# Laying out every engine's work anew in a planned attention + FFN kernel, with the planner's durations taken from a trace

## The chip, the cores and the metric

The kernel runs on one core of one Trainium2 chip. A core has five engines that run side by side, each working through its own instructions in the order in which they were written: TensorE (PE in the profile; PEld is its loading of weights, which overlaps), VectorE (DVE), ScalarE (ACT), GpSimd (POOL) and SyncE (SP), which here only issues DMAs. An instruction that waits for a semaphore holds up everything behind it on its engine. The metric is the device time of one launch in microseconds (us); lower is better. Before the change it is 315.80 us, the median of three runs (315.71 to 315.86).

## The reference

Attention in which a query sees only the keys of its own cluster, then a gated feed-forward network (FFN). There are 4 batches of 8 heads with 768 positions of 64 values, 16 centroids for each head; the FFN goes from 512 to 1536 and back on 3072 tokens.

```python
q_assign = np.argmax(np.einsum('bhsd,hcd->bhsc', q_n, c_n), axis=-1)
k_assign = np.argmax(np.einsum('bhsd,hcd->bhsc', k_n, c_n), axis=-1)
mask = q_assign[:, :, :, None] == k_assign[:, :, None, :]
scores = np.where(mask, scale * np.matmul(q, k.transpose(0, 1, 3, 2)), -1000000000.0)
...
attn = attn / (np.sum(attn, axis=-1, keepdims=True) + 1e-09)
x = np.matmul(attn, v)  # heads side by side: 3072 x 512
gate = 1.0 / (1.0 + np.exp(-(x @ w_gate)))
val = x @ w_val
out = gate * val @ w_out
```

## The kernel before

**The work of one pair of heads.** Heads go in pairs p = 0 to 3 of each batch b. Queries, keys and values come in by DMA (`dma`, line 323) into nine tiles "nat". Queries and keys are turned so that the 64 values lie on the partitions: in batch 0 and the first pairs of batch 1 by TensorE transposes (lines 881 for pair 0, 773 for pairs 1 to 3 of batch 0, 595 for pairs 0 and 1 of batch 1) whose result DVE or ACT copies out of PSUM (L555 on DVE, L780 on ACT), otherwise by DVE in blocks (`turn_blocks`, L573). TensorE then scores them against the centroids in float32 (L926, L813; L665 for two pairs at a time). DVE turns these scores (L527), takes the largest (L534), matches it (L541: which centroid has the largest score) and turns the one-hot rows back, straight into the operands as mask rows (L552) or into a tile that DMAs spread. POOL casts the turned queries and keys to float16 (L801, L628, L895) into "even" and "odd" tiles; from batch 1 on a DMA shifts the second head's half into "odd" (L632). The operands have 80 rows then: 64 values and 16 one-hot rows, so that one matmul gives score and mask together. POOL also casts the values (L499).

**Attention** (`attend`). The scores of a unit (L986, 256 or 384 columns) go into one of two PSUM buffers "sc"; ACT takes the exponential of a whole buffer (L1010, 768 or 1024 elements) into one of four "es" tiles; TensorE multiplies these with the values and a column of ones (L1037, 65 columns), which gathers in one PSUM buffer "av" the sums and their divisor. At the end of a block of queries DVE takes the reciprocal (L1062) and multiplies (`norm`, L1067) into "xn", which is turned into x by a DMA transpose on SP (L1095) or by TensorE (L1075) with a copy by DVE (L1091).

**FFN** (`feed`, `project`). For each half of a batch's tokens, 12 steps of a gate and a value product (L1372: four matmuls each, into three PSUM buffers "ring"), a tanh on ACT in place of the sigmoid (L1390), and DVE's product into hT (L1401). The output projection is done on 2 by 2 blocks with seven products (L1252), with sums of weights (L1145 to L1151, DVE), of hT (L1221, DVE), and scalings and sums of the products (L1277 ACT, L1283, L1287, L1325 DVE, L1298 ACT, L1304 and L1308 POOL). The FFN of one half runs between the attention of later ones, so that TensorE always has something.

**What sets the order.** Nothing is emitted where it stands in the code. Each piece is a task: engine, duration, what it waits for, the buffers that it takes and uses, a due time, an earliest time, and `lat`, which is how long after its end its readers may start. `Order.schedule` plans all engines together in the planner's own time. On each engine, of the tasks that could start within 0.02 us of the first, the one with the smallest due time goes next:

```python
first = min(c[0] for c in cand)
start, t = min(
    (c for c in cand if c[0] <= first + 0.02), key=lambda c: (c[1].due, c[0])
)
```

The planned starts are the order in which the instructions are emitted, and so the order of each engine's queue and the choice of buffers. On the chip only this order remains: durations and due times have no effect of their own. Due times come from `due_at(slot)` for attention (a slot is a score unit, 96 in batch 0) and `due_ffn(work)` for the FFN (`work` counts its TensorE time); the many small offsets (for instance 3.5 and -23.5 at the value product) move one kind of task against another.

Of the kernel before, what the change touches and what calls it, by code (L numbers as in the profile page):

```python
# [12 lines left out]
ALU = mybir.AluOpType  # L13
# [187 lines left out]
def kernel(  # L201
# [204 lines left out]
    c4 = od.add("DVE", 1.65, c_scale, [c1], due=-8.8, seq=[c2])  # L406
# [85 lines left out]
    def load_v(b, p, eng, due, due_cast, early=0.0, behind=()):  # L492
        i = b * NP + p
        load_nat(b, p, "v", eng, due, early, behind=behind)
        buf = natb[b, p, "v"]
        vload[b, p] = [
            od.add(
                "POOL", 0.5,
                lambda e=e: nc.gpsimd.tensor_copy(  # L499
                    vps[i % NVP][:, e, :, 0:D], buf.tile[:, e, :, :]  # L500
                ),
                nat[b, p, "v"] + [ones[i % NVP]] + last_av.get((i - NVP, e), []),
                due_cast, uses=[buf],
            )
            for e in range(2)
        ]
# [50 lines left out]
    def prepare(b, grp, due, step, act=(), queues=("SP",), split=False):  # L557
# [5 lines left out]
        for p, nm in sides:  # L563
            t32[p, nm] = Buf("t32")
            for half in range(2):
                if quarters(b, p):

                    def turn_blocks(p=p, nm=nm, half=half):
# [10 lines left out]
                        "DVE", 0.55, turn_blocks, nat[b, p, nm], due, lat=0.15,  # L579
# [20 lines left out]
                def copy(p=p, nm=nm, half=half, rb_=rb_):  # L600
# [11 lines left out]
                    "ACT" if (nm, half) in act else "DVE", 0.5, copy,  # L612
                    [tr], due, lat=0.15, uses=[rb_, t32[p, nm]],
# [4 lines left out]
        for p in grp:  # L618
            ev, od_ = aug[b, p] = Buf("even"), Buf("odd")
            prev = []  # L620
            for half in (0, 1) if split else (None,):
# [13 lines left out]
                for nm in ("k", "q"):  # L635
                    first = not prev and not c
                    c.append(
                        od.add(
                            "POOL", 0.83 * part, lambda nm=nm, cast=cast: cast(nm),
                            [cp[p, nm, h] for h in hs], due, seq=(prev + c)[:1],  # L640
                            acq=[ev] if first else [],
                            uses=[t32[p, nm]] + ([] if first else [ev]),
                        )
                    )
# [29 lines left out]
        for half in range(2):  # L674
# [10 lines left out]
            def back(cols=cols, oh=oh, half=half):  # L685
# [4 lines left out]
                "DVE", 0.53,  # L690
                lambda t1=t1, half=half: turn_scores(take(t1)[:n], rg.tile[:n, half, :QB]),
                [cl], due, acq=[t1], uses=[rg],
            )
            a2 = od.add(
                "DVE", 0.52,
                lambda t1=t1, mx=mx: top_scores(take(mx)[:n], t1.tile[:n]),
                [a1], due, acq=[mx], uses=[t1], lat=0.0,
            )
            a3 = od.add("DVE", 0.55, same, [a2], due, acq=[oh], uses=[t1, mx], lat=0.0)
            if quarters(b, grp[0]):  # L700
                a3 = od.add("DVE", 0.25, weigh, [a3, c_small], due, uses=[oh], lat=0.0)
            a5 = od.add(
                "DVE", 0.38, back, [a3], due, seq=turned[-1:],
# [24 lines left out]
    def place(b, p, ohf, tiles, last, due, alloc, c):  # L728
# [6 lines left out]
        for n_, (e, nm, h) in enumerate(rows):  # L735
            g = tiles.index((nm, h))
            m = od.add(
                "DVE", 0.395,
                lambda g=g, e=e, nm=nm, h=h: turn_matches(
                    aug[b, p][e].tile[64:96, NM[nm], h * QB : (h + 1) * QB],  # L740
                    ohf.tile[32 * g : 32 * g + 32, 32 * e : 32 * e + QB],
                ),
                [last, *alloc], due + 0.3 * n_ + (0.0 if n_ > 5 else 0.0), uses=[ohf, aug[b, p][e]],
            )
            masked[b, p, e, nm, h] = [c[nm, e, h], m]
# [11 lines left out]
    def prepare_pair(b, p, due, step, act=("q",), direct=False):  # L757
# [3 lines left out]
        for h in range(2):  # L761
            for nm in ("k", "q"):
# [15 lines left out]
                def copy(nm=nm, cols=cols, rg=rg):  # L778
# [12 lines left out]
                    "ACT" if nm in act else "DVE", 0.5, copy, [tr], due, lat=0.15, uses=[rg, t32[nm]]  # L791
# [4 lines left out]
        for nm, e in (("k", 0), ("q", 0), ("k", 1), ("q", 1)):  # L796
            to = od_ if e else ev

            def cast(nm=nm, e=e, to=to):
# [4 lines left out]
                "POOL", 0.83, cast, [cp[nm, 0], cp[nm, 1]], due + 0.1 * e,  # L804
# [58 lines left out]
    def prepare_first(due):  # L863
# [8 lines left out]
        for nm, h in (("k", 0), ("k", 1), ("q", 0), ("q", 1)):  # L872
# [34 lines left out]
            cp[nm, h] = od.add(on, 0.5, copy, [tr], due, lat=0.1, uses=[rg, t32[nm]])  # L907
# [30 lines left out]
        for dur, go, acq, uses in (  # L938
            (0.58, lambda: turn_scores(take(t1), rg.tile[:, :QB]), t1, [rg]),
            (  # L940
                0.55,
# [19 lines left out]
    def attend(block, at, slot):  # L961
# [13 lines left out]
        early = slot < 108.0  # L975
# [28 lines left out]
        def exponentials():  # L1004
# [16 lines left out]
            "ACT", 0.13 + 0.00078 * together * N, exponentials,  # L1021
            [*t1, c_small, c3], due, lat=0.2, acq=[es], uses=[sc],
# [8 lines left out]
        def value():  # L1031
# [15 lines left out]
            due + (-4.1 if last else 3.5) - (23.5 if early else 0.0), lat=0.25 if last else 0.0,  # L1047
# [52 lines left out]
        t4 = od.add("DVE", 0.17 + 0.02 * nq, rec, [t3], due - 18.0, lat=0.05, acq=[rr], uses=[av])  # L1100
        t5 = od.add("DVE", 0.14 + 0.15 * nq, norm, [t4], due - 18.0, lat=0.2, acq=[xn], uses=[av, rr])
        if not ((b, gr) == (0, 0) and p >= 2 or (b, p) == (0, NP - 1) or block == blocks[-1]):
# [3 lines left out]
                    "SP", 1.4, turn_by_dma, [t5], due - 18.0, seq=xd[:1], lat=0.0 if b else 5.0, dma=0.4,  # L1106
# [4 lines left out]
        t6 = od.add("PE", 0.02 + 0.06 * nq, turn, [t5, c_ident16], due - 18.0, lat=0.25, acq=[rg], uses=[xn])  # L1111
        xd.append(
            od.add(
                "DVE", 0.1 + 0.133 * nq, out_of_bank, [t6], due - 18.0, lat=0.2, seq=xd[:1],
# [12 lines left out]
    def sum_weights(due):  # L1127
# [26 lines left out]
        for kind, dur in (("1112", 0.84), ("2122", 0.84), ("1122", 0.42)):  # L1154
# [10 lines left out]
    def project(b, one, two, final, many, end):  # L1165
# [45 lines left out]
        def add(to, place, x, y, op, behind=()):  # L1211
            tasks = []
            for n, (i0, i1) in enumerate(parts):
# [4 lines left out]
                        "DVE", 0.15 + 0.067 * (i1 - i0),  # L1218
# [7 lines left out]
                        due - -10.0 - (6.0 if end and not n else 0.0), lat=0.15, acq=fresh,  # L1226
# [16 lines left out]
        def product(ring, bank, new, lo, hi, left_, right, deps, acq, uses, n0=0, runs=((0, NFC // 2),)):  # L1243
# [33 lines left out]
            "ACT", 0.4, first(fresh_hf, lambda: nc.scalar.mul(t_hf(), t_r1()[:, HM:], 0.5)), [m2], due, lat=0.2,  # L1277
# [4 lines left out]
            "DVE", 0.42,  # L1282
# [4 lines left out]
            "DVE", 0.42, lambda: stt(t_hf(), t_r2()[:, HM:], 0.5, t_df()[:, 1], ALU.mult, ALU.add),  # L1287
# [6 lines left out]
        def mixed():  # L1294
# [3 lines left out]
            "ACT", 0.6, lambda: nc.scalar.mul(mixed(), t_r1(), 0.5), [m5, m4], due_ffn(work()), lat=0.2,  # L1298
# [4 lines left out]
            eng, 0.42 if eng == "DVE" else 0.65,  # L1303
# [4 lines left out]
            eng, 0.42 if eng == "DVE" else 0.65, lambda: add_on.tensor_tensor(t_df()[:, 0], t_df()[:, 0], t_hf(), ALU.add),  # L1308
# [12 lines left out]
        if not end:  # L1321
            m7 = product(r2, t_r2, False, 0, HM, lambda: a(0, 1), lambda i: views["2122"][:, i], a7, [], hs)
            e5 = od.add(
                "DVE", 0.68,
# [10 lines left out]
            "DVE", 0.42, lambda: stt(o2.tile[:, 1, HM:], t_r2()[:, HM:], 0.5, t_df()[:, 1], ALU.mult, ALU.add),  # L1335
# [9 lines left out]
        for lo, hi in zip(cuts, cuts[1:]):  # L1345
# [5 lines left out]
                "DVE", 0.12 + 0.3 * (hi - lo) / HM,  # L1351
# [7 lines left out]
    def feed(b, gr, work):  # L1359
# [24 lines left out]
        for fc in range(NFC):  # L1384
# [4 lines left out]
                "ACT", 0.12 + 0.3 * w,  # L1389
# [3 lines left out]
                [g1, c3], due, lat=0.2, acq=[gt], uses=[rg],  # L1393
# [4 lines left out]
            def gated(fc=fc, rv=rv, gt=gt):  # L1398
# [8 lines left out]
                    "DVE", 0.1 + 0.4 * w, gated, [g2, v1], due - 15.0, lat=0.2, seq=done[:1],  # L1407
# [12 lines left out]
        if not wsum_done:  # L1420
            sum_weights(93.0)
# [22 lines left out]
    for p_ in range(1, NP):  # L1444
# [17 lines left out]
    for p_ in range(1, NP):  # L1462
        prepare_pair(0, p_, (0, 9.5, 13.5, 18.5)[p_], 0.24, (('k', 'q'), (), ('k', 'q'))[p_ - 1], p_ in (1, 2, 3))
# [75 lines left out]
```

## Time and profile before

| what | value |
|---|---|
| median of 3 runs | 315.80 us (315.71 to 315.86) |
| the profiled execution's own time | 315.89 us |
| its span | 314.1 us, so 1.8 us lie around it |
| PE busy | 307.8 us (98%), 3083 matmuls |
| ACT busy | 221.3 us (70%) |
| DVE busy | 206.0 us (66%) |
| POOL busy | 93.4 us (30%) |
| DMA | 36.83 MB, mean 117 GB/s |
| granted TensorE clock | 0.999 |

A line of the timeline reads: start in us, duration, engine, line and operation, output<-inputs, shape and type, how many in a row, and in brackets the idle time before it with what ended it. In the chain that ended last a line is start, length and what ran. Matmuls overlap their neighbours, so the length of one is longer than what it costs in a row; the start-to-start step of equal matmuls is the cost. A queue's lines (SPq) are DMAs, with the time the engine spent to issue them, waits included.

### The profile page before, as it was taken

How to read it: one execution, taken by the hardware profiler on the slowest of the kernel's cores; microseconds unless marked ns; L12 is line 12 of the kernel's file. 1: busy time of each engine (PE TensorE's matmuls, PEld its weight loads, DVE VectorE, ACT ScalarE, POOL GpSimd, SP SyncE). 2: the span in 40 equal slices, each digit the busy share in tenths (PEclk: the TensorE clock that was granted, in tenths of full speed). 3: DMA queues.
4: the chain of work that ended last, by engine and by line, in shares of the span. 5: the costliest groups of instructions: out<-in, count | busy, mean ns of one | idle time of the engine just before them, and what ended most of it. 6: DMA issues, size and time to landing. Idle time of an engine off the chain costs nothing.

```text
span 314.1 us, 7876 instructions
## 1 busy us (share of the span) xinstructions
PE 307.8 (98%) x3083; PEld 213.3 (68%) x3083; DVE 206.0 (66%) x480; ACT 221.3 (70%) x323; POOL 93.4 (30%) x140
## 2 busy tenths in 40 slices
PE   8999999999999999999999999999999999999995
PEld 4567888545668866567666876657766787667674
DVE  4999733899979659485335899576333753457684
ACT  4699999237999767777788857767788777632321
POOL 4998659551014224420202135430210021000000
PEclk9999999999999999999999999999999999999999
DMA  6999999957175669521574649631310012000103
GB/s 221 374 220 251 216 211 168 187 121 131 42 114 88 143 121 263 147 77 37 120 113 71 103 78 234 176 83 40 88 57 13 15 61 100 3 0 12 58 2 134
DMA packets 79957, 36.83 MB, mean 117 GB/s; under 512 B 64512, under 2 KB 74864, under 8 KB 79920
## 3 DMA queue, kind: packets, MB, share of 16 engines
q1 hardware_dynamic: 72048, 24.30, 33.1%
q0 software_dynamic: 6864, 11.01, 17.6%
q10 hardware_dynamic: 1008, 1.02, 0.9%
q8 instruction: 24, 0.39, 0.5%
q14 instruction: 13, 0.11, 0.1%
HBM read 28.34 MB, written 6.29 MB: 110 GB/s over the span
## 4 chain that ended last, share of the span: by engine, by line
PE 91%; DVE 7%; issue 1%; ACT 0%; DVEq 0%; ACTq 0%
PE ring L1372 40%; PE sc L986 18%; PE ring L1252 14%; PE av L1037 10%; PE sc L665 3%; PE sc L1252 3%; DVE even L552 2%; DVE odd L552 1%; PE av L348 1%; DVE t L527 1%; DVE ohf L541 1%; PE ring L881 1%; DVE mx L534 1%; DVE t L555 1%; PE ring L595 1%
## 5 line engine op out<-in xcount | busy, mean ns | idle before, releaser
L1010 ACT ACTIVATE es<-sc,nbias 128x768 f16<-128x768 f32 (+1 forms) x189 | 167.1, 913 | 34.6 <-PE sc L986 33.1
L1401 DVE SCALAR_TENSOR_TENSOR hT<-gt,ring 128x384 f16<-128x384 f32 (+2 forms) x96 | 53.0, 552 | 58.9 <-PE ring L1372 55.0
L1372 PE MATMUL ring<-x,wv 128*128 128x384 f16 (+2 forms) x384 | 78.1, 326 | 0.0
L1372 PE MATMUL ring<-x,wg 128*128 128x384 f16 (+2 forms) x384 | 78.1, 326 | 0.0
L1390 ACT ACTIVATE gt<-ring 128x384 f32<-128x384 f32 (+2 forms) x96 | 47.1, 490 | 35.1 <-PE ring L1372 20.9
L1037 PEld LDWEIGHTS <-es 128*128 128x128 f16 x1152 | 55.1, 97 | 17.6
L1037 PE MATMUL av<-vp,es 128*128 128x65 f16 x1152 | 60.2, 193 | 0.0
L1372 PEld LDWEIGHTS <-wv 128*128 128x128 f16 x384 | 34.7, 98 | 20.7 <-issue 0.6
L1372 PEld LDWEIGHTS <-wg 128*128 128x128 f16 x384 | 34.5, 97 | 19.6 <-issue 0.2
L628 POOL CAST even<-t 128x768 f16<-128x768 f32 x24 | 20.1, 839 | 70.2 <-DVE t L573 60.1
L1252 PEld LDWEIGHTS <-hT 128*128 128x128 f16 x294 | 27.1, 98 | 4.6 <-issue 0.6
L1304 POOL TENSOR_TENSOR diff<-out 128x256 f32<-128x256 f32 x9 | 7.5, 834 | 70.4 <-ACT out L1298 70.4
L986 PE MATMUL sc<-even 80*128 80x384 f16 (+2 forms) x120 | 26.7, 293 | 1.5 <-DVE even L552 0.7
L986 PEld LDWEIGHTS <-odd 80*128 80x128 f16 x216 | 19.9, 98 | 10.1 <-issue 2.5
L986 PE MATMUL sc<-odd,even 80*128 80x384 f16 x96 | 26.5, 326 | 0.1
L986 PEld LDWEIGHTS <-even 80*128 80x128 f16 x216 | 19.8, 98 | 9.8 <-issue 1.9
L986 PE MATMUL sc<-even,odd 80*128 80x384 f16 (+2 forms) x120 | 26.1, 293 | 0.1
L986 PE MATMUL sc<-odd 80*128 80x384 f16 x96 | 25.9, 325 | 0.0
L499 POOL CAST vp<-nat 128x384 f16<-128x384 f32 x32 | 17.0, 570 | 18.5 <-DMA nat<-in_v_dram 14.9
L573 DVE STREAM_TRANSPOSE t<-nat 128x384 f32<-128x384 f32 x40 | 20.9, 551 | 0.0
L1252 PEld LDWEIGHTS <-s 128*128 128x128 f16 x180 | 16.7, 98 | 3.3 <-DVE diff L1283 0.6
L1067 DVE TENSOR_TENSOR xn<-av,rr 128x384 f16<-128x384 f32 (+2 forms) x36 | 18.3, 509 | 0.9
(113 smaller groups left out, 315.3 us busy)
## 6 DMA issues: line engine op xcount, KB each, us to landing
out_dram<-out SPq DMA_DIRECT2D x21, 256.0 KB, 2.6
nat<-in_v_dram POOLq DMA_DIRECT2D x12, 384.0 KB, 4.5
nat<-in_k_dram SPq DMA_DIRECT2D x32, 96.0 KB, 2.9
nat<-in_q_dram SPq DMA_DIRECT2D x32, 96.0 KB, 3.0
odd<-even SPq DMA_DIRECT2D x12, 192.0 KB, 4.5
nat<-in_k_dram SPq DMA_DIRECT2D x5, 384.0 KB, 5.9
nat<-in_q_dram SPq DMA_DIRECT2D x5, 384.0 KB, 5.8
nat<-in_v_dram SPq DMA_DIRECT2D x4, 384.0 KB, 7.3
```

The source lines that it names most:

```text
L499: lambda e=e: nc.gpsimd.tensor_copy(vps[i % NVP][:, e, :, 0:D], buf.tile[:, e, :, :]),
L552: nc.vector.transpose(to.bitcast(FP), of.bitcast(FP))
L573: nc.vector.transpose(t[:, half * QB : (half + 1) * QB].rearrange("p (c x) -> p c x", x=128), blocks_[:, half],)
L628: nc.gpsimd.tensor_copy(t[:, NM[nm], cols], t32[p, nm].tile[:, cols])
L986: nc.tensor.matmul(out=to, lhsT=kb.tile[0:80, 0, e * QB + j // 2 * 128 : e * QB + (j // 2 + 1) * 128], rhs=qb_.tile[0:80, 1, e * QB + c0 * ...
L1010: i = nc.scalar.activation(to, of, AF.Exp, bias=nbias, scale=D ** -0.5 if quarters(b, p) else scale,).ins
L1037: nc.tensor.matmul(out=av.tile[:, g : g + D + 1], lhsT=es.tile[:, i * N + c * 128 : i * N + (c + 1) * 128], rhs=vp[:, e, j, :], start=firs ...
L1067: nc.vector.tensor_tensor(take(xn)[:, :nq].rearrange("p c (e d) -> p (c e) d", d=D), sums()[:, :, 0:D], rr.tile[:, : 2 * nq].unsqueeze(2). ...
L1252: nc.tensor.matmul(out=ps[:, lo:hi], lhsT=left_()[:, i], rhs=right(i)[:, n0 : n0 + w], start=new and i == 0, stop=i == NFC // 2 - 1, skip_ ...
L1372: nc.tensor.matmul(out=ps[:, :N], lhsT=ws[fc // FPG][:, dcc, fc % FPG, :], rhs=xb.tile[:, dcc, :N], start=(dcc == 0), stop=(dcc == NDC - 1),)
L1390: lambda rg=rg, gt=gt: nc.scalar.activation(take(gt)[:, :N], rg.tile[:, :N], AF.Tanh, scale=0.5),
L1401: nc.vector.scalar_tensor_tensor(t[:, fc, :N], gt.tile[:, :N], 1.0, rv.tile[:, :N], ALU.add, ALU.mult)
```

## The change

Every instruction stays. What changes is what the planner is told, and so the order of the tasks on each engine and which buffer each gets:

- Durations and `lat` of nearly all DVE, ACT and POOL tasks get other values. The sum of both changes less: the exponential of 768 elements goes from 0.73 + 0.20 to 0.78 + 0.16, `norm` for three chunks from 0.59 + 0.20 to 0.46 + 0.14, the POOL cast from 0.83 to 0.865, the tanh of 384 from 0.42 + 0.20 to 0.38 + 0.16.
- Due times: attention of batch 0 advances by 0.403 a slot in place of 0.414; the FFN by 1.78 for each us of work in place of 1.82; value products get +5.5 in place of +3.5, and early ones (slots under 132, before under 108) -19.5 in place of -23.5 besides; early scores keep -32.5, for slots under 132 now; reciprocal, `norm` and what follows get -13 in place of -18; the sums of hT +11 in place of +10; `gated` -14 in place of -15.
- The preparation of pair 1 and of the later batches, the weight loads (`WT`), the loads of values (due and earliest times) and the first loads of batch 1's keys and queries (earliest 18.5 in place of 17.5) are moved.

The diff, cut to its core:

```diff
-        return T1 + (slot - S1) * (0.414 if slot < S1 else 0.826)
+        return T1 + (slot - S1) * (0.403 if slot < S1 else 0.826)
...
-        return 36.0 + work * 1.82
+        return 36.0 + work * 1.78
...
-                "POOL", 0.5,
+                "POOL", 0.46,
                 lambda e=e: nc.gpsimd.tensor_copy(
                     vps[i % NVP][:, e, :, 0:D], buf.tile[:, e, :, :]
...
-                        "DVE", 0.55, turn_blocks, nat[b, p, nm], due, lat=0.15,
+                        "DVE", 0.48, turn_blocks, nat[b, p, nm], due, lat=0.1,
...
-            a3 = od.add("DVE", 0.55, same, [a2], due, acq=[oh], uses=[t1, mx], lat=0.0)
+            a3 = od.add("DVE", 0.5, same, [a2], due, acq=[oh], uses=[t1, mx], lat=0.1)
...
-            (0.55, lambda: top_scores(take(mx), t1.tile), mx, [t1]),
-            (0.67, same, oh, [t1, mx]),
+            (0.59, lambda: top_scores(take(mx), t1.tile), mx, [t1]),
+            (0.83, same, oh, [t1, mx]),
...
-        early = slot < 108.0
+        early = slot < 132.0
...
-            "ACT", 0.13 + 0.00078 * together * N, exponentials,
-            [*t1, c_small, c3], due, lat=0.2, acq=[es], uses=[sc],
+            "ACT", 0.147 + 0.00083 * together * N, exponentials,
+            [*t1, c_small, c3], due, lat=0.16, acq=[es], uses=[sc],
...
-            due + (-4.1 if last else 3.5) - (23.5 if early else 0.0), lat=0.25 if last else 0.0,
+            due + (-4.1 if last else 5.5) - (19.5 if early else 0.0), lat=0.25 if last else 0.0,
...
-        t4 = od.add("DVE", 0.17 + 0.02 * nq, rec, [t3], due - 18.0, lat=0.05, acq=[rr], uses=[av])
-        t5 = od.add("DVE", 0.14 + 0.15 * nq, norm, [t4], due - 18.0, lat=0.2, acq=[xn], uses=[av, rr])
+        t4 = od.add("DVE", 0.11, rec, [t3], due - 13.0, lat=0.12, acq=[rr], uses=[av])
+        t5 = od.add("DVE", 0.12 + 0.113 * nq, norm, [t4], due - 13.0, lat=0.14, acq=[xn], uses=[av, rr])
...
-                    "SP", 1.4, turn_by_dma, [t5], due - 18.0, seq=xd[:1], lat=0.0 if b else 5.0, dma=0.4,
+                    "SP", 1.4, turn_by_dma, [t5], due - 13.0, seq=xd[:1], lat=0.0 if b else 5.0, dma=0.4,
...
-                "ACT", 0.12 + 0.3 * w,
+                "ACT", 0.036 + 0.345 * w,
...
-                    "DVE", 0.1 + 0.4 * w, gated, [g2, v1], due - 15.0, lat=0.2, seq=done[:1],
+                    "DVE", 0.06 + 0.405 * w, gated, [g2, v1], due - 14.0, lat=0.14, seq=done[:1],
...
-        load_v(0, p_ - 1, "SP", -7.8 + p_, 16.0 + 4.5 * p_, behind=nat[0, p_, "q"])
-    load_v(0, NP - 1, "SP", -7.7 + p_, 16.0 + 4.5 * NP, behind=nat[0, NP - 2, "v"])
-    WT = (11.0, 16.0, 23.0, 21.0, 28.5, 29.5, 40.0, 30.0, 43.0)
+        load_v(0, p_ - 1, "SP", -7.8 + p_, 20.0 + 4.5 * p_, behind=nat[0, p_, "q"])
+    load_v(0, NP - 1, "SP", -7.7 + p_, 20.0 + 4.5 * NP, behind=nat[0, NP - 2, "v"])
+    WT = (12.5, 16.0, 23.0, 24.0, 29.5, 29.5, 40.0, 30.0, 43.0)
...
-        prepare_pair(0, p_, (0, 9.5, 13.5, 18.5)[p_], 0.24, (('k', 'q'), (), ('k', 'q'))[p_ - 1], p_ in (1, 2, 3))
+        prepare_pair(0, p_, (0, 10.0, 13.5, 18.5)[p_], 0.24, (('k', 'q'), (), ('k', 'q'))[p_ - 1], p_ in (1, 2, 3))
...
-                            due - 60 if b else 38.0 if grp[0] else 17.5,
+                            due - 60 if b else 38.0 if grp[0] else 18.5,
...
-                prepare(b + 1, grp, max(due - 27.5, 41.5) + (9.5 if (b, grp[0]) == (0, 2) else 0), 1.26)
+                prepare(b + 1, grp, max(due - 27.5, 45.5) + (9.0 if (b, grp[0]) == (0, 2) else 0), 1.33)
...
-                    load_v(b + 1, p_, "POOL", due - 32.0, due - 15, due - 17.5)
+                    load_v(b + 1, p_, "POOL", due - 32.0, due - 15, due - 12.5)
```

More of the change, by code (lines that the diff above doesn't have):

```diff
@@ L405 @@
     )
-    c4 = od.add("DVE", 1.65, c_scale, [c1], due=-8.8, seq=[c2])
+    c4 = od.add("DVE", 1.84, c_scale, [c1], due=-8.8, seq=[c2])
     c_ring = Buf("av")
@@ L611, in prepare @@
                 cp[p, nm, half] = od.add(
-                    "ACT" if (nm, half) in act else "DVE", 0.5, copy,
-                    [tr], due, lat=0.15, uses=[rb_, t32[p, nm]],
+                    "ACT" if (nm, half) in act else "DVE", 0.475, copy,
+                    [tr], due, lat=0.11, uses=[rb_, t32[p, nm]],
                 )
@@ L638, in prepare @@
                         od.add(
-                            "POOL", 0.83 * part, lambda nm=nm, cast=cast: cast(nm),
+                            "POOL", 0.865 * part, lambda nm=nm, cast=cast: cast(nm),
                             [cp[p, nm, h] for h in hs], due, seq=(prev + c)[:1],
@@ L790, in prepare_pair @@
                 cp[nm, h] = od.add(
-                    "ACT" if nm in act else "DVE", 0.5, copy, [tr], due, lat=0.15, uses=[rg, t32[nm]]
+                    "ACT" if nm in act else "DVE", 0.375 if nm in act else 0.475, copy, [tr], due, lat=0.15 if nm in act else 0.11, uses=[rg, t32[nm]]
                 )
@@ L906, in prepare_first @@
             turns.append(tr)
-            cp[nm, h] = od.add(on, 0.5, copy, [tr], due, lat=0.1, uses=[rg, t32[nm]])
+            cp[nm, h] = od.add(on, 0.375, copy, [tr], due, lat=0.16, uses=[rg, t32[nm]])
             rows = [
@@ L1334, in project @@
         e5 = od.add(
-            "DVE", 0.42, lambda: stt(o2.tile[:, 1, HM:], t_r2()[:, HM:], 0.5, t_df()[:, 1], ALU.mult, ALU.add),
+            "DVE", 0.335, lambda: stt(o2.tile[:, 1, HM:], t_r2()[:, HM:], 0.5, t_df()[:, 1], ALU.mult, ALU.add),
             [m6, e2], due_ffn(work()), lat=0.2, uses=[r2, df, o2],
```

52 lines of the change are left out of this document (26 added, 26 removed).

## Prediction

> **What bounds the kernel now.** I read the page's busy shares and the chain that ended last, then the windows of 10 us, then the timeline where the windows show TensorE waiting.
>
> ```profile
> PE 307.8 (98%) x3083; PEld 213.3 (68%) x3083; DVE 206.0 (66%) x480; ACT 221.3 (70%) x323; POOL 93.4 (30%) x140
> PE 91%; DVE 7%; issue 1%; ACT 0%; DVEq 0%; ACTq 0%
> ```
>
> TensorE is the bound: 98% busy, 91% of the chain. No matmul is added, dropped or reshaped, so only its waiting can change. Busy time includes overlap of neighbours, so I measured waiting by steps, from the start of one matmul to the start of the next. The chain gives the step of a 384-column matmul: 13.00/80 = 0.1625 us.
>
> ```profile
> 288.39 13.00 PE ring L1372 x80
> ```
>
> In the same way 512 columns step 0.216, 256 columns 0.109 and six value-product matmuls 0.19. All steps add up to about 303.7 us. The first matmul starts at 0.77 and the last ends at 310.57, so TensorE waits about 6 us in all: 2.8 before 12.5 us, 3.1 between 12.5 and 38, 0.25 near 55 to 58 (0.09 at 55.8, 0.16 at 58.4), and nothing after that. The windows agree (columns: window and its length, then busy us and instructions of PE, its weight loads, DVE, ACT and POOL, the granted clock, the DMA share, GB/s): PE lacks a few tenths up to 40 us and nothing later.
>
> ```profile
> 10.00:20.00 10.00, 9.43 (x102) 6.01 (x101) 9.47 (x24) 8.12 (x12) 9.70 (x14) 1.00 1.12 327
> 20.00:30.00 10.00, 9.40 (x137) 7.63 (x135) 9.38 (x25) 9.53 (x12) 9.60 (x14) 1.00 1.15 231
> 30.00:40.00 10.00, 9.56 (x142) 8.20 (x141) 7.33 (x19) 9.94 (x13) 6.08 (x9) 1.00 1.23 213
> 40.00:50.00 10.00, 10.00 (x139) 8.43 (x137) 3.89 (x11) 10.00 (x16) 6.61 (x10) 1.00 1.13 181
> 80.00:90.00 10.00, 10.00 (x100) 5.87 (x98) 8.28 (x20) 9.94 (x14) 0.00 (x0) 1.00 0.36 69
> ```
>
> The 3.1 us between 12.5 and 38 are a dozen waits. By steps the large ones are 0.60 at 31.23 (an exponential), 0.43 at 22.43 (an exponential), 0.41 at 28.80 (a mask row on DVE), 0.23 at 14.72 (an exponential); the rest are 0.08 to 0.22. The timeline shows the two engines behind them: ACT, with a hole before 15.43 because its es buffers wait for the value product at 15.04, and DVE's chain for the masks of the last head pair, which ends with the mask row at 28.33 that releases the score at 28.80.
>
> ```profile
> 15.04 0.53 PE L1037 MATMUL av<-vp,es 128*128 128x65 f16 x12
> 15.43 2.48 ACT L1010 ACTIVATE es<-sc,nbias 128x768 f16<-128x768 f32 x3 [0.76 <-PE av L1037]
> 21.21 0.74 DVE L541 TENSOR_TENSOR ohf<-t,mx 128x384 f16<-128x384 f32 x1
> 26.80 0.88 DVE L541 TENSOR_TENSOR ohf<-t,mx 128x384 f16<-128x384 f32 x1
> 28.33 0.37 DVE L552 STREAM_TRANSPOSE even<-ohf 32x192 f32<-32x192 f32 x1
> 28.80 0.49 PE L986 MATMUL sc<-even 80*128 80x256 f16 x3 [0.25 <-DVE even L552]
> 31.23 0.27 PE L986 MATMUL sc<-even 80*128 80x256 f16 x1 [0.44 <-ACT es L1010]
> ```
>
> **The change, part by part.** I compared the order on each engine in the two kernels. Of 942 TensorE groups 183 neighbours change places and none moves over 22 places. Steps depend on the shapes of neighbours; counted with the steps above the new adjacency is worth under 0.1 us, taken as nothing. Until 13.1 us TensorE's order is the same: 2.8 us of waiting stay. The end is the same too (last matmul 310.57, last store lands 312.92).
>
> *14 to 20 us.* Four value-product groups go ahead of scores and of transposes. They free es buffers sooner: ACT's hole of 0.76 shrinks to about 0.45, and exponentials up to 28 us run 0.3 to 0.5 earlier. But whatever TensorE saves here (up to the 0.43 at 22.43 and 0.23 at 14.72) it waits again at 28.80, since DVE has no gap from 8.15 to 31 and its mask chain keeps its order from 18.42 on. Worth nothing, unless that chain ends earlier.
>
> *The mask chain.* On POOL the cast of the last pair's v, 1.29 us at 26.76, moves seven places up, ahead of the casts of that pair's even and odd tiles, to about 21.6.
>
> ```profile
> 26.76 1.29 POOL L499 CAST vp<-nat 128x384 f16<-128x384 f32 x2
> ```
>
> It stood beside the match at 26.80 (0.88). The same match took 0.57 at 9.36 with POOL idle, and 0.71 at 14.34 and 0.74 at 21.21 beside other casts. So the chain may shorten by 0.31 at most; and the cast now lies where the 21.21 match is, which may rise from 0.74 to 0.88, 0.14 later. Bounds: -0.31 to +0.14. I take the middle, -0.08, because DMA issues on POOL take the old place and neither end has a row of its own. The Trainium skill, *SBUF — State Buffer*, section "SBUF: two separate sides", says a DVE instruction with two SBUF inputs and a GpSimd one share a port pair as an exclusive lock held for the whole instruction. The trace agrees (0.57 alone, 0.88 beside the cast); by it the gain would be the whole 0.31 if the cast misses both matches. The v cast's own load landed at 17.29, so it waits for nothing; the pair's even and odd casts queue behind it some 0.5 later, still ahead of the masks that their scores need at 28.80.
>
> *28.8 to 38 us.* One score (29.69) goes ahead of a value group worth 0.25 (8 by 0.031). ACT's exponential behind it, after an idle of 0.66 at 30.06, starts 0.25 earlier, and since ACT is full from there to 55 (9.94 and 10.00 of 10), the 0.60 at 31.23 shrinks by it: **-0.25**. Its bounds are 0 (the mask row is late again) and -0.60 (the whole wait).
>
> *Key and query loads of batch 1 on SP.* A DMA transpose of x, issued at 17.95 because it waits for a norm, now stands ahead of the first key load, which goes from 9.95 to about 19.5 to 19.9.
>
> ```profile
> 9.95 0.37 SPq L323 DMA_DIRECT2D nat<-in_k_dram  x1
> 17.95 1.96 SPq L1095 DMA_TRANSPOSE x<-xn  x1
> 20.01 0.53 SPq L323 DMA_DIRECT2D nat<-in_q_dram  x1
> 25.05 0.82 PE L595 MATMUL ring<-ident,nat 128*128 128x128 f32 x6
> ```
>
> It is needed by the L595 transposes, about 26.3 in the new order. Loads issued at 20.01, 20.63 and 21.85 took 5.2, 5.9 and 5.8; the one at 9.95 took 8.3 behind a fuller queue. So it lands at 25.1 (by 5.2) to 28.2 (by 8.3). I take 25.3, since its new neighbours in time are the 5.2 and 5.9 rows: hidden, cost nothing. The three loads behind it land some 1.1 later (the spacing of 25.25, 26.52, 27.65), the first at about 26.3 for a transpose at 28.06, also hidden. The Trainium skill, *DMA: Bandwidth & Descriptors*, section "Issuing engines are not separate DMA queues", says that DMAs of all issuers interleave on the same 16 engines; the weight loads of POOL at 13.12 and 16.27 landed at 21.06 and 24.01 here, so by it the load could be slower than the 5.2.
>
> *40 to 60 us.* TensorE's order is the same up to 55. Then two FFN groups go ahead of the first centroid scores (L665), an xn transpose takes another ring buffer and the 0.16 at 58.4 goes, but the next 512-column group waits about 0.1 for the copy (L1091) behind one transposing turn (L573): **-0.05**, between -0.16 and +0.36 (a whole turn of 0.46 more).
>
> *60 to 80 us.* The second L665 group (70.59) goes 1.7 earlier; its eight DVE turns, which ended at 69.82, go ahead in DVE's order and end at about 67.6 for a need at 68.4: margin 0.8. Five FFN groups go ahead of batch 1's first scores (72.03 to 74.2). The eight mask rows' DMAs stand behind two shifts on SP, issue from about 69.3 and land from 71.2: margin 2. Nothing waits. A v load on POOL goes behind the first L628 cast at 61.25; its tile is not read before 88.
>
> *80 to 275 us.* Attention runs 2 to 3 us later against FFN and projection; the median TensorE work between a pair of scores and its value product rises from 2.66 to 3.51 us, so an exponential may be later than before without being waited for. On the other side the closest waits are score buffers, 0.04 to 0.15 us of margin at 80 and 85 us, and norms, 0.27 at 96 and 108. Before ran margins of 0.0 at 81.4 and 83.5 without a wait, so I put 0, with +1.5 as the bound (five to ten such places by 0.15 to 0.3).
>
> *Sum.* On the profiled execution (span 314.1, time 315.89): -0.25 - 0.05 - 0.08 = -0.38, so 315.51. It was 0.09 above the median of 315.80, so **315.4** against the median.
>
> **The rivals.**
>
> A, faster: DVE's chain ends 0.31 earlier (the v cast misses both matches, as at 9.36). Then the time ACT won before 28 us is no longer thrown away: 0.31 at 28.80, 0.25 at 31.23, and the 0.15 at 34.03 and 0.09 at 37.28 go too, with 0.05 at 58: 0.85, so 315.80 - 0.85 = 314.95. For: each of those waits names ACT or that chain. Against: the cast may only have moved from one match to another.
>
> B, slower: the first key load of batch 1 lands late. At 8.3 us from 19.6 it lands at 27.9, 1.6 after its need; the transposes stand in TensorE's order with everything behind them, and less the 0.4 won: 317.0. It decides when the landing passes 26.3. For: weight loads took nearly 8 us from 13.12 and from 16.27. Against: 5.2 to 5.9 for three loads issued at 20 to 22.
>
> C, slower: the thin margins at 78 to 108 us fail, 1.0 to 1.5 in small waits: 316.4 to 316.9, taken as 316.6. For: ACT is 9.94 of 10 there, so a delay is passed on. Against: no wait anywhere after 60 us before.
>
> D, nothing comes of it: the moved cast costs the 0.14 at 21.21 and the exponential at 30.06 still waits: 315.8.
>
> **How the numbers follow.** Likeliest with D: 0.42, the own range 315.0 to 315.9. A 0.36, B 0.11, C 0.11. What a measurement can tell from no change is about 0.2%, 0.63 us: faster is below 315.17 (A), slower above 316.43 (B and C), 0.22. The low end 314.8 takes in A at 314.95 and some more; the high end 316.6 takes in C's middle; left out are B, C's upper half and a tail of A, 0.2.
>
> **What would show it.** Right: the score now at 28.80 still waits for a mask row, the wait at 31.23 is about 0.35, ACT's hole at 15.4 is about 0.45, no L595 group waits for DMA near 26, no TensorE wait appears after 60 us. A shows as a match near 26.5 of 0.57 and no wait for a mask row. B shows as a wait for the key load; C as releasers ACT or DVE ahead of scores and value products between 78 and 108. I am wrong altogether if steps of TensorE itself lengthen, or if loads of a later batch come late because attention lags behind.

## The result: slower by 0.1 to 0.2%, and the profile after

The changed kernel takes 316.38 us in the median of 12 executions (316.09 to 317.49), the kernel before 315.76 beside it: a ratio of 1.0023, 95% interval 1.0013 to 1.0033. In a second set of 12 it took 316.14 against 315.74, a ratio of 1.0009 (0.9997 to 1.0021). So it is slower by 0.6 us in the first set and by 0.4 in the second, whose interval just takes in no change; 0.4 faster was forecast. The profiled execution is one of the long ones: 317.11 us, span 315.3. Its busy shares and the chain that ended last:

```profile
PE 306.6 (97%) x3083; PEld 211.9 (67%) x3083; DVE 202.8 (64%) x480; ACT 220.8 (70%) x323; POOL 92.8 (29%) x140
PE 84%; POOL 5%; DMA 4%; DVE 4%; issue 1%; ACT 1%; SPq 1%; DVEq 0%; ACTq 0%
```

TensorE is still the bound, but POOL and DMA have entered the chain, which had neither in its list of engines before. The windows of 10 us that answer to those shown before, with two more behind them:

```profile
10.00:20.00 10.00, 9.03 (x105) 5.94 (x104) 9.21 (x25) 8.24 (x12) 9.73 (x14) 1.00 1.12 305
20.00:30.00 10.00, 9.21 (x137) 7.46 (x136) 9.39 (x25) 9.80 (x13) 9.73 (x14) 1.00 1.14 248
30.00:40.00 10.00, 9.67 (x147) 8.38 (x145) 6.94 (x19) 10.00 (x13) 5.61 (x8) 1.00 1.23 212
130.00:140.00 10.00, 9.25 (x88) 5.15 (x87) 5.94 (x14) 5.86 (x9) 2.57 (x5) 1.00 0.45 116
180.00:190.00 10.00, 9.50 (x110) 6.99 (x109) 6.26 (x10) 6.09 (x8) 3.85 (x5) 1.00 0.50 81
```

The last two are the news: before, PE was busy for 10.00 of 10 in both. The list of waits (engine and tile, what it waited for, us in total, times, longest) names them:

```profile
PE sc L986 <- DMA odd<-oht: 0.8, 1, 0.8
PE av L1037 <- POOL vp L499: 0.7, 1, 0.7
PE sc L986 <- ACT es L1010: 0.6, 2, 0.3
PE ring L1252 <- DVE diff L1283: 0.5, 1, 0.5
PE sc L986 <- POOL odd L801: 0.5, 1, 0.5
```

To count exactly, I took for each group of matmuls the time at which it starts less the steps of all groups ahead of it, with the steps of the prediction. What is left is the waiting so far. By stage, in us:

| stage | before | changed, this profile | changed, a second profile | both places mended (below) |
|---|---|---|---|---|
| to 12.5 us (same order) | 2.78 | 2.52 | 2.66 | 2.34 |
| 12.5 to 54 | 3.11 | 3.06 | 2.74 | 2.78 |
| 54 to 120 | 0.56 | 0.21 | 0.23 | 0.22 |
| 120 to 160 | 0.05 | 0.98 | 0.03 | 0.05 |
| 160 to 220 | 0.11 | 1.04 | 1.06 | 0.31 |
| 220 to the end | 0.05 | 0.05 | 0.05 | 0.03 |
| sum | 6.66 | 7.86 | 6.77 | 5.73 |
| time of that execution | 315.89 | 317.11 | 316.04 | 315.01 |

The sums differ as the times do (+1.20 beside +1.22, +0.11 beside +0.15, -0.93 beside -0.88), so nothing is hidden in the matmuls themselves. From 12.5 to 120 us the change wins 0.40 in one profile and 0.70 in the other, 0.33 to 0.35 of it behind 54 us. Then it loses 0.85 at two places in a projection, 177.6 (0.20) and 184.55 (0.65), and in this execution 0.84 more at 133.03. These are the waits themselves; the stages differ by some hundredths more.

**The place at 184.** The timeline of the changed kernel, DVE, then POOL, then TensorE:

```profile
179.28 2.61 DVE L1221 TENSOR_TENSOR s<-hT 128x768 f16<-128x768 f16 x3
181.81 1.55 DVE L1221 TENSOR_TENSOR hT<-hT 128x768 f16<-128x768 f16 x2
183.29 0.68 DVE L1325 SCALAR_TENSOR_TENSOR out<-ring,diff 128x512 f32<-128x512 f32 x1
184.07 0.42 DVE L1283 SCALAR_TENSOR_TENSOR diff<-ring,half 128x256 f32<-128x256 f32 x1
...
179.42 1.07 POOL L628 CAST even<-t 128x768 f16<-128x768 f32 x1 [4.02 <-DVE t L573]
180.46 1.02 POOL L1304 TENSOR_TENSOR diff<-out 128x256 f32<-128x256 f32 x1
181.56 0.92 POOL L1308 TENSOR_TENSOR diff<-diff,half 128x256 f32<-128x256 f32 x1
...
184.55 0.81 PE L1252 MATMUL ring<-wo,s 128*128 128x256 f16 x6 [0.50 <-DVE diff L1283]
```

A sum of hT on DVE steps by 0.46 us alone (two start at 176.20 and 176.66) and takes 0.55. Of the five here, three start while POOL's cast or sums run and take 1.17, 1.08 and 1.08. So L1325 and behind it L1283 come late, and the product needs L1283. Before, the sums were as slow (1.18, 1.08, 1.08, then 0.55), but a centroid group of 1.43 us and two scores stood between the products on TensorE, so that L1283 still ended 0.48 ahead of its product:

```profile
182.43 1.54 DVE L1221 TENSOR_TENSOR hT<-hT 128x768 f16<-128x768 f16 x2
185.19 0.41 DVE L1283 SCALAR_TENSOR_TENSOR diff<-ring,half 128x256 f32<-128x256 f32 x1
...
184.23 0.33 PE L986 MATMUL sc<-odd,even 80*128 80x384 f16 x1
184.39 0.32 PE L986 MATMUL sc<-odd 80*128 80x384 f16 x1
184.65 1.50 PE L665 MATMUL sc<-t,cblk 128*32 128x384 f32 x16
186.08 0.83 PE L1252 MATMUL ring<-wo,s 128*128 128x256 f16 x6
```

The new order put only two scores and a value group there, 0.5 us, and the centroid group behind.

**The place at 177.** Here two sums that stood behind L1283 before now stand directly ahead of it, and a third ahead of these, at 174.63, started while POOL cast and took 1.18 (0.55 before, at 175.82). Before, L1283 ended 0.22 ahead of its product.

```profile
176.20 1.01 DVE L1221 TENSOR_TENSOR hT<-hT,hT 128x768 f16<-128x768 f16 x2
177.13 0.41 DVE L1283 SCALAR_TENSOR_TENSOR diff<-ring,half 128x256 f32<-128x256 f32 x1
177.60 0.82 PE L1252 MATMUL ring<-wo,s 128*128 128x256 f16 x6
```

**The place at 133.** SP's queue before, then in the changed kernel, then the score that waits:

```profile
123.92 1.22 SPq L323 DMA_DIRECT2D even<-oht  x2
125.23 1.21 SPq L1095 DMA_TRANSPOSE x<-xn  x1
126.50 1.21 SPq L323 DMA_DIRECT2D odd<-oht  x2
```

```profile
124.18 0.50 SPq L632 DMA_DIRECT2D odd<-even  x1
125.35 1.22 SPq L1095 DMA_TRANSPOSE x<-xn  x1
126.66 1.61 SPq L323 DMA_DIRECT2D even<-oht  x2
128.32 1.22 SPq L323 DMA_DIRECT2D odd<-oht  x2
...
133.03 0.34 PE L986 MATMUL sc<-even,odd 80*128 80x384 f16 x1 [0.75 <-DMA odd<-oht]
```

Of the eight mask rows of batch 2 (odd<-oht and even<-oht) two stood first in this stretch before (123.92), the others behind the transpose. Now a shift and a DMA transpose stand ahead of them, the transpose waits for its norm until 125.35, and behind it the rows run into a 384 KB load of v that POOL issued at 127.97. The row of 128.32 landed at 132.99, after 4.67 us; before, the one of 126.50 took 1.85.

### The profile page after: what moved, and what is told of

Read it like the earlier page. It is cut to its first block, busy times and chain, and to the rows that moved or that the text cites. A ratio compares the mean times of both kernels' runs of the same rounds, so it can differ in the third digit from the quotient of the medians.

```text
span 315.3 us, 7880 instructions
## 1 busy us (share of the span) xinstructions
PE 306.6 (97%) x3083; PEld 211.9 (67%) x3083; DVE 202.8 (64%) x480; ACT 220.8 (70%) x323; POOL 92.8 (29%) x140
## 4 chain that ended last, share of the span: by engine, by line
PE 84%; POOL 5%; DMA 4%; DVE 4%; issue 1%; ACT 1%; SPq 1%; DVEq 0%; ACTq 0%
PE ring L1372 38%; PE sc L986 17%; PE ring L1252 13%; PE av L1037 9%; PE sc L665 3%; PE sc L1252 3%; POOL odd L801 2%; DMA odd<-oht 1%; DVE s L1221 1%; POOL even L801 1%; DMA nat<-in_q_dram 1%; POOL vp L499 1%; DMA cn<-in_centroids_dram 1%; ACT es L1010 1%; PE ring L595 1%
## 5 line engine op out<-in xcount | busy, mean ns | idle before, releaser
L628 POOL CAST even<-t 128x768 f16<-128x768 f32 x24 | 20.8, 867 | 74.1 <-DVE t L573 61.4
L986 PE MATMUL sc<-even 80*128 80x384 f16 (+2 forms) x120 | 26.0, 294 | 1.4 <-ACT es L1010 0.6
L1062 DVE RECIPROCAL rr<-av 128x6 f32<-128x6 f32 (+2 forms) x36 | 6.7, 185 | 21.2 <-PE av L1037 20.9
```

What stands on the lines that cost most here:

```text
L628: nc.gpsimd.tensor_copy(t[:, NM[nm], cols], t32[p, nm].tile[:, cols])
L986: nc.tensor.matmul(out=to, lhsT=kb.tile[0:80, 0, e * QB + j // 2 * 128 : e * QB + (j // 2 + 1) * 128], rhs=qb_.tile[0:80, 1, e * QB + c0 * ...
```

## The experiments

Times are medians of 6 to 12 executions, each with its ratio to the kernel before on the same chip. Lines are those of the kernel run; where an edit adds lines, L1221 is L1228 and so on.

**The changed kernel again.** No edit.

> The changed kernel as it is, once more. Theory 1: its profile (317.11 us) lost 0.20 us at 177.6 and 0.65 at 184.55 because DVE's L1283 comes late, and 0.84 at 133.03 because mask rows queue behind a v load. The first two hang on the order of one engine's queue and stand in every execution; the third hangs on the race of two DMAs and is there in some. So in an execution near 316.2 I expect the waits at 177.6 and 184.6 again, within 0.15 us of their size, and the one at 133 absent or under 0.3. Rival: the waits are scatter of one execution; then those at 177.6 and 184.6 are gone or elsewhere. Median by both 316.1 to 316.6.

316.14 us (316.00 to 316.84), ratio 1.0009 (0.9997 to 1.0021). The profile (316.04) has 0.20 at 176.5 and 0.65 at 183.45 again, to the hundredth, and no wait at 132: the row that the score needs went out 0.05 us after POOL's v load and landed at 130.98; in the first profile it went out 0.35 after it and landed at 132.99. So the projection's waits belong to the order; the one at 133 is a race, won here with about 1.0 us to spare (score at 131.96) and lost by 0.84 in the first profile. Whether all executions above 316.5 come of that race stays open: the kernel before has a few (317.05, 317.52) too.

**The v loads set back.**

```diff
-                    load_v(b + 1, p_, "POOL", due - 32.0, due - 15, due - 12.5)
+                    load_v(b + 1, p_, "POOL", due - 32.0, due - 15, due - 17.5)
```

> The changed kernel with only the earliest time of the later batches' v loads set back (due - 17.5 in place of due - 12.5), so that batch 1's third v load stands two places earlier on POOL, ahead of the last two casts. Theory 1: it has landed before the mask rows are issued, no execution has the wait at 133, none is near 317, median 316.1 to 316.2; the waits at 177.6 and 184.6 stay. Rival (the attention simply trails, and what is not waited for here is waited for behind): the 0.84 turns up at another place, median unchanged at 316.4 or more.

316.93, ratio 1.0034 (1.0022 to 1.0046): a miss. The load now went out at 123.86, but with the same SP queue ahead the first row, issued at 126.53, landed at 131.66 and its score waited 0.50 at 131.98. This does not clear the load: set back, it was issued ahead of all the rows and landed at 130.75. It shows that an earlier load is no remedy as long as the rows are issued this late, which leaves SP's order to try. The number also moved work elsewhere: at 181.34 a value product waited 1.42 for a norm (L1067) behind one of the slow sums.

**Two sums behind L1283.**

```diff
...
+        if b == 1:
+            od.behind(a6[0], closing[-1:])
+            od.behind(a7[0], [e2])
...
```

Here `closing` holds the L1325 of the pairs before, and e2 is L1283.

> The changed kernel with two of DVE's sums of hT (L1221) of batch 1's projections put behind L1325 and L1283. Theory 1: L1283 no longer stands behind them, the waits at 177.6 and 184.6 go, 0.85 us less: 315.4 to 315.6 in median, with some executions 0.8 higher from the DMA wait at 133. Rival: L1283 is late because of what feeds it (ACT's L1277, POOL's L1308) or the two sums are then late for their own products, and at most 0.2 is won: 316.1 or more.

315.84 (315.52 to 316.51), ratio 1.0001 (0.999 to 1.0011). The wait at 177 is gone, that at 184 is 0.33 in place of 0.65, as one sum still stood ahead of L1283: 0.49 less waiting from 160 to 220 us, and 0.3 to 0.5 in the median. Less than I expected, for a reason that the profile shows, and below the rival's 316.1.

**Both edits.**

> The v loads set back and the two sums put behind, together. Theory 1: what is left of the change is its gain up to 60 us, some 0.3 to 0.5: 315.3 to 315.5, no execution above 316. Rival (time only moves): 316.0 or more.

316.01, ratio 1.0004 (0.9994 to 1.0014), where the rival had put it: the wait for the norm stands at 180.13 with 0.65. The v loads' number is no remedy.

**The v cast put back on POOL.**

```diff
+    for t in vload[0, NP - 1]:
+        od.behind(t, list({id(m[0]): m[0] for key, m in masked.items() if key[:2] == (0, NP - 1)}.values()))
```

> The changed kernel with the cast of the last pair's v (1.29 us before, now at 21.5) put back behind that pair's four casts on POOL; nothing else moves. Theory 2 (up to 31 us DVE's chain of masks sets the pace, whatever TensorE saves before it waits for it): the 0.64 us wait at 25.6 for POOL's L801 goes, the wait for a mask row near 28.6 grows from 0.17 by about the same, and the sum of waits up to 30 us stays at 4.7 to 4.9: median within 0.2 of the changed kernel's 316.1. Rival (the wait at 25.6 is a loss of its own): 0.4 to 0.64 us less, 315.5 to 315.7.

316.43 (316.24 to 316.63), ratio 1.0021 (1.0012 to 1.003). Nothing is won, but the run does not decide between the two, since the wait that it was to take away did not go. It stands at 25.45 with the same 0.64, and the profile now names another releaser. First the changed kernel, then this one:

```profile
25.59 0.49 PE L986 MATMUL sc<-even 80*128 80x256 f16 x3 [0.50 <-POOL odd L801]
```

```profile
25.45 0.49 PE L986 MATMUL sc<-even 80*128 80x256 f16 x3 [0.50 <-ACT es L1010]
26.61 0.87 DVE L541 TENSOR_TENSOR ohf<-t,mx 128x384 f16<-128x384 f32 x1
```

POOL's cast had only ended last by chance; the score waits for an exponential to free its buffer. In the kernel before, six transposes (25.05, L595) filled that gap, and the change moved them behind. The second line is the price of the old place: the match takes 0.87 again, where it took 0.56 in the changed kernel.

Theory 2 is not borne out either, and the median is 0.33 above its 316.1, where 0.2 was allowed. The later match did not make the wait near 28.6 grow: it is 0.18 at 28.69, as before this edit at 28.83, and the later chain shows only as 0.15 at 29.41. In the changed kernel the mask row for that score ends at 28.38, and the score starts 0.14 after the first of these exponentials, which ends at 28.69:

```profile
27.57 5.32 ACT L1010 ACTIVATE es<-sc,nbias 128x1024 f16<-128x1024 f32 x5
28.01 0.37 DVE L552 STREAM_TRANSPOSE even<-ohf 32x192 f32<-32x192 f32 x1
28.83 0.49 PE L986 MATMUL sc<-even 80*128 80x256 f16 x3
```

The waits at 25.59 and, in this run, at 25.45 and 28.69 end 0.14 after an exponential too, and ACT works without a hole from 22.5 to 31 us in the changed kernel. So at these scores it is ACT's exponentials that hold TensorE, not DVE's chain.

**The mask rows ahead on SP.** The rows get an earlier due time, and the shift and the transpose go behind them.

```diff
...
-                                [a5, shifted[b, p, half]], due - (20.0 if (b, grp[0]) == (1, 0) else 0),
+                                [a5, shifted[b, p, half]], due - (20.0 if (b, grp[0]) in ((1, 0), (2, 0)) else 0),
...
+                            sent.setdefault((b, grp[0]), []).append(m)
...
+                if (b, grp[0]) == (2, 2):
+                    od.behind(d, sent[2, 0])
...
+            if (b, gr, p) == (1, 1, 2):
+                od.behind(xd[-1], sent[2, 0][:2])
```

> The changed kernel with the eight mask rows of batch 2's first pairs put back ahead of one shift and one DMA transpose on SP, as they stood before the change. Theory 1b (after the run with earlier v loads: SP's order, not the v load, makes these rows land at 131 to 134 where their score stands at 131.5): the rows are issued from 124.2, the first land by 129, no wait near 132 in any execution, so none of those at 316.5 and above: median 315.9 to 316.1, the waits at 177 and 184 stay. Rival (the queues are full there and the rows land at 131 or later all the same): scatter and median as the changed kernel's, 316.1 to 316.4.

316.13 (315.98 to 316.37, and one of 317.72), ratio 1.0017 (1.0007 to 1.0026). Rows issued from 124.32, the first four landed by 128.20, no wait near 132; 0.20 and 0.65 stay. The median hardly moves, so the race was not lost in most of the changed kernel's executions. No execution above 316.5 was expected and one came, so not every long one is this race.

**Rows ahead, and the sums behind L1283** (at 184 both of them).

```diff
+            od.behind(a6[0], [e2] if len(closing) == 5 else closing[-1:])
+            od.behind(a7[0], [e2])
```

> The mask rows put ahead as in the run before, and DVE's sums of batch 1 put behind L1283 as in the run with later sums, at 184 both of them (there L1283 had still come 0.33 late, behind one sum). By theory 1 all three waits are gone and the gain before 60 us is left, 0.3 to 0.6: 315.2 to 315.4, against 315.75 of the kernel before. Rival (a wait that goes lets the next through): 315.7 or more.

315.31 (315.01 to 315.57), ratio 0.9986 (0.9978 to 0.9995): as expected, and faster than both kernels. DVE and TensorE at the place:

```profile
181.15 0.69 DVE L1335 SCALAR_TENSOR_TENSOR out<-ring,diff 128x512 f32<-128x512 f32 x1 [0.62 <-POOL diff L1318]
181.94 0.42 DVE L1290 SCALAR_TENSOR_TENSOR diff<-ring,half 128x256 f32<-128x256 f32 x1
182.28 0.55 DVE L1228 TENSOR_TENSOR hT<-hT 128x768 f16<-128x768 f16 x1
...
182.16 0.35 PE L1041 MATMUL av<-vp,es 128*128 128x65 f16 x6
182.42 0.81 PE L1259 MATMUL ring<-wo,s 128*128 128x256 f16 x6
```

By the steps the product (182.42) waits less than 0.1 in place of 0.65. The two sums, now past POOL's work, take 0.55 each; in the changed kernel the first of them took 1.08 and the second 0.55.

**The planner told a longer sum.** The changed kernel told it 0.46 for a sum of six parts, the kernel before 0.55.

```diff
-                        "DVE", 0.076 + 0.064 * (i1 - i0),
+                        "DVE", 0.55 + 0.064 * (i1 - i0),
```

> The changed kernel with one number set otherwise: the planner is told 0.93 us for a sum of hT of 6 parts (0.55 + 0.064 each) in place of 0.46, near what these sums take beside POOL's work in the traces (1.07 to 1.18) and far from what they take alone (0.55). It then lays a centroid group (L665) between the products at 184 again, as before the change, and L1283 ahead of the later sums. Theory 1c (the loss at 177 and 184 comes of the duration told, which holds only where POOL is idle): both waits go, 0.8 less than the changed kernel, 315.3 to 315.5; the mask rows at 132 still come late in some executions. Rival (133 of TensorE's groups change places, new waits stand where these were): 315.8 or more.

317.79, ratio 1.0059 (1.0043 to 1.0075). The centroid group is back between the products, and there is no wait from 133 to 190, but the rival's new waits came: 0.25 at 191, 0.46 at 249.8, and most of all at the last projection. POOL is idle there, yet it was laid out for slow sums too: 0.74 told for sums of three parts, which take 0.35. It waits 1.31 at 306:

```profile
305.42 0.89 DVE L1221 TENSOR_TENSOR nat<-hT 128x384 f16<-128x384 f16 x3
305.82 0.88 PEld L1252 LDWEIGHTS <-nat 128*128 128x128 f16 x9 [1.42 <-DVE nat L1221]
305.83 0.50 PE L1252 MATMUL sc<-wo,nat 128*128 128x256 f16 x3 [1.14 <-DVE nat L1221]
```

**The same, with the shift alone put behind the rows.**

> The same with the mask rows put ahead of the shift on SP. Theory 1c: 315.2 to 315.4, as the kernel with both places mended by hand (315.31). Rival: 315.8 or more.

317.53, ratio 1.0053 (1.0037 to 1.007), the same wait at 305.71.

**Told long for batch 1 alone.**

```diff
+                        "DVE", (0.55 if b == 1 else 0.076) + 0.064 * (i1 - i0),
```

> The long duration told only for batch 1's sums, the only ones with POOL's work beside nearly all of them; the others keep the 0.46. In the run before, with 0.93 everywhere, the waits at 177 and 184 were gone, but 0.33 came at 303.6 and 1.31 at 306.2, at the last projection, where POOL is idle and a sum takes 0.55 as the changed kernel was told. Theory 1d (the duration has to be that of the place): order as there from 150 to 200 us and as the changed kernel's elsewhere, waits at 177, 184, 303 and 306 all gone; an exponential waited for at 191 (0.25) may stay: 315.4 to 315.8, with some executions higher from the mask rows at 132. Rival (the rearranged stretch passes the wait on): 316.0 or more.

315.58 (315.42 to 316.58), ratio 1.0 (0.9991 to 1.0009). Waits at 177, 184, 303 and 306 are gone, 0.25 at 191 stays. One number brings 0.6 to 0.8 against the changed kernel's 316.1 to 316.4. But it is not a true duration of the place: in the changed kernel 4 of batch 1's 15 sums take over 1 us, as 2 of batch 0's do, and in this kernel one, at 173.61; the other 14 take 0.51 to 0.56. Told long, the sums are spread out, most of them lie past POOL's work, and L1283 comes in time. The number works as slack. None of the runs puts back the old 0.55, so what in the change took the cover away, this number or a due time, stays open.

**The same, with the shift alone put behind the rows.**

> The same with the mask rows put ahead on SP. Theory 1d: 315.3 to 315.6, near the kernel with both places mended by hand (315.31). Rival: 316.0 or more.

315.53 (315.35 to 316.21), ratio 0.9991 (0.9982 to 1.0). In its profile (316.21) the transpose still stands ahead on SP, the rows go out from 126.63 as in the changed kernel, and 0.65 is waited for at 132.81.

**Told long for batch 1, shift and transpose behind the rows.**

> The long duration told for batch 1's sums, and the mask rows ahead of both the shift and the DMA transpose of x. In the run before only the shift was put behind the rows; the transpose still stood ahead of them and waited for its norm until 125.3, the rows were issued from 126.6 as in the changed kernel, and 0.65 us was waited for them at 132.8. Theory 1e (the transpose that waits is what holds the rows): rows issued from 124.2, no wait at 132 in the profile, no scatter upwards: 315.1 to 315.4. Rival (the rows land late by the load on the queues): a wait of 0.3 or more at 132, 315.5 or more.

315.43 (315.13 to 315.85), ratio 0.9983 (0.9974 to 0.9992). SP, with the rows from 124.15, and the score without a wait:

```profile
124.15 1.25 SPq L323 DMA_DIRECT2D even<-oht  x2
125.45 1.21 SPq L323 DMA_DIRECT2D odd<-oht  x2
...
131.37 0.33 PE L990 MATMUL sc<-even,odd 80*128 80x384 f16 x1
```

So it is the transpose, waiting for its norm on SP, that holds the rows; the shift alone is not enough.

## Why the prediction was wrong

**The step that failed is "80 to 275 us", put at 0 with +1.5 as its bound.** It cost 0.85 in every profile of this order and 1.69 in the first, beyond the bound. The step looked for thin margins at score buffers and norms, at 78 to 108 us, and there nothing waits. It has no term for DVE's L1283, on which the projection's products wait, nor for batch 2's mask rows. I had put all of it at nothing because before had run on margins of 0.0. That does not carry over: at 184 the sums are as slow as before, but the centroid group that covered L1283 has gone; at 177 a sum lies otherwise beside POOL and two more have gone ahead of L1283. Rival C had about the right price (316.4 to 316.9 beside 316.38 and 316.14) and the wrong place, and a chance of 0.11.

**Mask rows.** I followed SP's queue for batch 1, where shifts also went ahead of rows, and found 2 us of margin. Nothing waited there, but the margin was not that: the rows went out from 69.33, as forecast, 0.63 behind a v load of POOL, and the first landed at 73.30 in place of 71.2, 0.87 ahead of its score at 74.17. The same move for batch 2 I did not follow. There a transpose that waits at the head of the queue comes on top. Loads of a later batch that come late are named in the prediction as a sign of being wrong, without a price.

**14 to 20 us: worth nothing, right, for a reason that does not hold.** ACT's hole was 0.85 in the first profile and 0.22 in the second, for 0.45 forecast: the value product that went ahead needs POOL's cast of v as well, and waited 0.83 and 0.20 for it. The waiting from 12.5 to 30 us is 2.18 before and 2.39, 2.07 after. But the score at 28.83 no longer waits for a mask row, as the prediction had it: an exponential holds it (above).

**The mask chain, -0.08 between -0.31 and +0.14: both ends came at once.** The match at 26.80 fell from 0.88 to 0.56, and the one at 21.05 rose from 0.74 to 0.91, together -0.15. Both signs of rival A came with it, a match of 0.56 and no wait for a mask row, but not its gain, since ACT then holds the score.

```profile
21.05 0.91 DVE L541 TENSOR_TENSOR ohf<-t,mx 128x384 f16<-128x384 f32 x1
26.80 0.56 DVE L541 TENSOR_TENSOR ohf<-t,mx 128x384 f16<-128x384 f32 x1
```

**28.8 to 38 us, -0.25:** the wait at 31.23 fell from 0.60 to 0.47, and the stage's waiting from 1.00 to 0.75, since in the first profile two small waits ahead of it (0.08 at 29.21, 0.14 at 30.41) went too; those at 34 and 37 only moved. (ACT's idle before 30.06, from which this term was worked out, is 0.48 in the trace and not 0.66.) Together from 12.5 to 54 us -0.05 in one profile and -0.37 in the other, for -0.33 forecast.

**The key load of batch 1:** issued at 18.75, landed at 24.47 (5.7 us), no transpose waited. Right; rival B did not occur. **40 to 60 us:** the 0.16 at 58.4 went, and the 0.10 expected behind it did not come. **60 to 80 us:** nothing waits over 0.1, right.

So the gain forecast, 0.38, was there or a little more: with the two later places mended the kernel is 0.4 us faster than before. That the size fits is in part luck. Behind 54 us 0.33 to 0.35 was won where 0.05 was forecast: besides the 0.16 at 58.4, small waits of the kernel before went (0.10 at 79.66, 0.07 at 90.58, 0.05 at 99.63) that the prediction had counted as nothing. In the first profile the stage from 12.5 to 54 us gave only 0.05. All of it and more was given back between 130 and 185 us.

## What to carry to other kernels

A duration read from a trace holds for the company in which the instruction ran: the sums of hT step by 0.46 alone and take over 1 us where they start beside POOL's work. One number for both is wrong somewhere: 0.46 was too short at 184, and the longer rule, 0.74 for half a sum, too long at 306. When an order is laid out anew, list for every wait that is zero today what covers it, and see whether the cover is still there, through the whole span and in every batch; a stage without waits is where the loss can come from. In a queue that works in order, ask of each DMA that waits what stands behind it, and do not trust a named releaser that ended only just before the wait.

## What the runs showed of the hardware

- Which of two contenders starts first decides who pays. At 14 us POOL's cast of v took 0.84 where DVE's match had started 0.08 before it (the next casts 0.50), and the value product waited 0.83; in the second profile the cast started 0.20 before the match, and the wait was 0.20, with the match at 0.70 in place of 0.56. The Trainium skill, *SBUF — State Buffer*, section "SBUF: two separate sides", says that whichever of the two starts first holds the shared ports for its whole instruction; these rows agree.
- The same holds for float16 sums with both inputs in SBUF. They take 0.51 to 0.56 alone or where they start first (0.55 at 253.16 in the kernel before, where POOL's sum came 0.03 later and took 1.10), and up to 1.19 where POOL's work was running when they started, in both kernels. The price can be read off: such a sum takes 0.41 more than what POOL's instruction still had to run. In the kernel before it took 0.80 with 0.39 left, 1.07 with 0.66, 1.18 with 0.77. The match goes by the same figure (0.70 with 0.29 left in the second profile, 0.88 with 0.48 at 26.80 before). So what a sum will cost follows from where it starts, and the sum moved past POOL's work fell from 1.08 to 0.55.
- The opening, in the same order, waited between 2.31 and 2.85 us up to 12.5 us in the profiles of all kernels. That spread of 0.54 is as large as what the change was worth. A difference of 0.3 us between two profiles says nothing until the stage is split off.
